# A prologue in pairs of token tiles, with attention units inside it, and a second norm in place on VectorE

## The chip, the cores and the metric

One core of a Trainium2 chip. The metric is the time on the device in microseconds, the median of several executions. The engines are named as in the profile: PE is TensorE's matmuls (PEld its weight loads), ACT is ScalarE, DVE is VectorE, POOL is GpSimd, SP is SyncE, which issues most of the DMAs.

## The reference

A block with S = 2048 tokens of D = 1024, 32 heads of 32, and an MLP of F = 3584 that gates the attention:

```python
xn = layernorm(x)                                     # first norm
q, k, v = split(xn @ wqkv)                            # 32 heads
s = softmax(q @ k.T * 32 ** -0.5) @ v @ wo            # "mha"
y = layernorm(xn)                                     # second norm
g = silu(gelu(y @ w1 + b1) @ w2 + b2)
out = x + s * g
```

Weights, inputs and the output are bfloat16.

## The kernel before

The kernel lists its operations in program order, and a small class finds for each the semaphores to wait on. What runs on one engine runs in the order of the list: the statistics of x stood on VectorE behind one small operation until 21.30 us.

The prologue works on four batches of four tiles of 128 tokens. All x tiles are loaded first, then the weights of K, Q and V for the first heads, and the halving of the bias `b2h` stands ahead of the statistics on VectorE:

```python
for tb in range(NT): ... dma_start(xst[tile tb], x2[tile tb])          # SyncE
load_wq(0)                                                             # three slices of 512 KB
...
op("gpsimd", dma_start(b2h, B_b2 ...), w=["b2"], dma="b2")
op("vector", tensor_scalar_mul(b2h, b2h, 0.5), r=["b2"], w=["b2"])
...
for tb in range(4): stat(tb)                     # two bn_stats and one bn_aggr, VectorE
for b in range(NT // 4):
    rstd(b); ...; nbias(b)                       # power of -1/2 on GpSimd
    for i in range(4): xnorm(4 * b + i) ...      # VectorE; between them stat of the next batch
    ycoef(b)                                     # small operations on GpSimd
    for i in range(4): ynorm(4 * b + i)          # GpSimd, then stored to DRAM
    for i in range(4): transp(4 * b + i)         # 8 transposes on TensorE, eviction to xnT on ScalarE
    run_now(qk_item(0, 1, 512 * b, 512)); ...    # K, four V, Q: 192 matmuls, evicted by ScalarE
load_piece(0); load_y(0)                         # first MLP weights; y, transposed by the DMA
```

(cut and shortened)

Then follow 512 attention units (8 groups of 4 heads, 8 query blocks, 8 key blocks). Each has 8 score matmuls, two exps of 128x1024 on ScalarE, and 16 matmuls for PV and the row sums. With each unit goes one *item* of other TensorE work, 28 to 32 matmuls: part of the MLP, a projection for the next heads, or, at the end, an output item (`wo_item`). The items share one PSUM bank, 7, so the next one starts only when the last one has been evicted by VectorE. Output items that are left after unit 511 run by themselves: the tail.

The softmax here doesn't subtract the row's maximum and nothing guards it: scores larger than these inputs give would overflow.

## Time and profile before

| | us |
|---|---|
| median of 4 runs (1173.06 to 1175.22) | 1173.76 |
| span of the profiled execution | 1170.1 |
| first exp / exp of unit 8 / exp of the last unit begin | 86.3 / 103.0 / 1131.0 |
| tail after the last exp begins | 39.1 |

The times of exps come from the trace's records of the 1024 exps in order; two make a unit, and the time given for a unit is the start of its first exp ("last" is unit 511). The page's row of 40 slices, each a fortieth of the span with its busy share in tenths, shows where there is slack:

```profile
PE   0789999999998999999999999999999999899998
ACT  0459999999999999999999999999999999999960
```

From the fourth slice on both engines are full, up to the tail. In the first slice TensorE does hardly anything, in the next two it is at 7 and 8 tenths, and ScalarE is not full before the fourth. The chain of waits, followed back from the last instruction to what each step waited for (start, duration, what; the kernel before), says why:

```profile
3.13 17.98 DMA b2h<-in_B_b_dram
21.13 0.17 DVE b2h L241
21.30 1.20 DVE stats L247 x2
...
38.34 9.40 PE ps L304 x145
48.37 3.72 ACT xnT L298 x4
52.13 8.83 PE ps L304 x192
...
90.25 1.94 ACT P L603 x2
...
1135.14 30.39 PE ps L304 x832
```

VectorE waits 18 us for the landing of a 4 KB bias, whose halving takes 0.17 us and whose result is needed only in the MLP; the statistics of x stand behind it. Projection begins at 38.34 us. Each batch then has matmuls, an eviction (left out), and 3.72 us in which ScalarE evicts the four transposed tiles; of these gaps of 4.4 us TensorE works for 1.9 (the transposes) and waits for 2.5. The last line is the tail: 26 output items of 32 matmuls, 1.17 us each.

The windows view gives the busy time of each engine in a stretch, with the count of instructions in brackets, then the granted clock, the DMA share and GB/s. Of the kernel before:

```profile
core 0: us, PE busy (x) PEld busy (x) DVE busy (x) ACT busy (x) POOL busy (x), PEclk, DMA share, GB/s
10.00:16.00 6.00, 0.00 (x0) 0.00 (x0) 0.00 (x0) 0.00 (x0) 0.00 (x0) 1.00 1.26 319
16.00:19.00 3.00, 0.00 (x0) 0.00 (x0) 0.00 (x0) 0.00 (x0) 0.00 (x0) 1.00 1.53 200
20.00:22.00 2.00, 0.00 (x0) 0.00 (x0) 0.87 (x3) 0.00 (x0) 0.00 (x0) 1.00 1.11 304
38.34:85.70 47.36, 39.79 (x868) 28.06 (x872) 19.36 (x36) 21.45 (x35) 22.22 (x29) 0.93 0.34 108
1131.45:1170.10 38.65, 34.78 (x960) 25.08 (x952) 31.13 (x63) 1.44 (x2) 0.73 (x1) 0.99 0.67 165
```

Three stretches of the front first: the DMAs move 319 GB/s while x (rows of 2 KB) loads, then 200 and 304 while the weights (rows of 512 bytes) do. In the projection TensorE is busy for 39.79 of 47.36 us at a clock of 0.93. One more reading is the group of the first normalizations on VectorE (line, operation, tile and shape, count; busy us, mean ns; idle before):

```profile
L279 DVE TENSOR_SCALAR hT<-OT,lnp 128x1024 bf16<-128x1024 bf16 x16 | 13.8, 880 | 6.2 <-PE ps L295 6.2
```

The mean of 880 ns mixes two kinds: some 500 ns, and 1170 ns (twice 1420) while GpSimd runs a `ynorm`.

### The profile page before, as it was taken

The numbers are of one execution on the slowest core, as the hardware profiler recorded it, in microseconds if no ns is written. First come the engines' busy times: TensorE is split into PE (matmuls) and PEld (weight loads), VectorE is DVE, ScalarE is ACT, GpSimd is POOL, SyncE is SP. The second block draws the span as 40 slices with busy tenths as digits, with TensorE's granted clock in tenths as the row PEclk, the third lists the DMA queues.
The fourth block names the chain that finished last, engine by engine and source line by source line (L and its number), as shares of the span: only waits on it lengthen the run. The fifth ranks groups of instructions, "written<-read, shape, count | busy, mean of one in ns | idle before, by whom it ended". The sixth has DMA issues, their size and how long they took to land.

```text
span 1170.1 us, 62673 instructions
## 1 busy us (share of the span) xinstructions
PE 1093.0 (93%) x29696; PEld 688.6 (59%) x29696; DVE 599.5 (51%) x1327; ACT 1054.9 (90%) x1281; POOL 88.2 (8%) x116
## 2 busy tenths in 40 slices
PE   0789999999998999999999999999999999899998
PEld 0555665566655666556666665566655566566666
DVE  2817665146682254764226675136673246742468
ACT  0459999999999999999999999999999999999960
POOL 1810000000000000000000000000000000000000
PEclk9999999999999999999999999999999999999999
DMA  9243226512245320433422225522145321752756
GB/s 198 110 122 105 62 80 170 161 60 75 75 125 159 113 80 4 146 102 103 133 64 77 76 87 144 174 87 76 51 127 155 115 72 50 227 150 78 134 139 173
DMA packets 198481, 129.87 MB, mean 111 GB/s; under 512 B 41552, under 2 KB 189008, under 8 KB 198224
## 3 DMA queue, kind: packets, MB, share of 16 engines
q1 hardware_dynamic: 193584, 125.85, 36.8%
q8 instruction: 232, 3.80, 1.3%
q0 software_dynamic: 4640, 0.02, 0.6%
q14 instruction: 25, 0.20, 0.1%
HBM read 104.87 MB, written 12.58 MB: 100 GB/s over the span
## 4 chain that ended last, share of the span: by engine, by line
PE 50%; ACT 42%; DVE 4%; DMA 3%; issue 2%; POOL 0%; SPq 0%; POOLq 0%
ACT P L603 37%; PE ps L304 30%; PE ps L591 8%; PE ps L620 7%; PE ps L623 5%; ACT th L404 3%; DMA b2h<-in_B_b_dram 2%; ACT xnT L298 1%; DMA war<-in_B_w_dram 1%; DVE stats L247 1%; DVE xb L396 1%; ACT thz L438 1%; DVE u L399 0%; DVE u L401 0%; DVE hT L279 0%
## 5 line engine op out<-in xcount | busy, mean ns | idle before, releaser
L603 ACT ACTIVATE P<-ps 128x1024 bf16<-128x1024 f32 x1024 | 984.6, 1103 | 18.7 <-PE ps L591 15.1
L620 PE MATMUL ps<-P,VP 128*32 128x256 bf16 x4096 | 262.9, 278 | 1.1 <-issue 1.0
L623 PE MATMUL ps<-P,ones 128*32 128x256 bf16 x4096 | 258.3, 273 | 1.6 <-issue 1.6
L304 PE MATMUL ps<-hT,war 128*32 128x352 bf16 (+1 forms) x5376 | 230.2, 308 | 8.6 <-issue 7.1
L304 PE MATMUL ps<-yTc,war 128*32 128x352 bf16 (+1 forms) x5376 | 225.9, 308 | 10.6 <-issue 5.0
L591 PE MATMUL ps<-QT,KT 32*128 32x256 bf16 x4096 | 204.2, 273 | 9.1 <-ACT P L603 5.1
L304 PEld LDWEIGHTS ps<-yTc,war 128*32 128x32 bf16 x5376 | 139.3, 97 | 57.8 <-issue 9.6
L620 PEld LDWEIGHTS ps<-P,VP 128*32 128x32 bf16 x4096 | 107.8, 95 | 111.0 <-issue 98.8
L304 PEld LDWEIGHTS ps<-hT,war 128*32 128x32 bf16 x5376 | 141.7, 97 | 50.7 <-issue 9.5
L396 DVE TENSOR_SCALAR xb<-ps,b1T 128x352 f32<-128x352 f32 (+1 forms) x168 | 96.1, 572 | 131.1 <-PE ps L304 130.1
L591 PEld LDWEIGHTS ps<-QT,KT 32*128 32x128 bf16 x4096 | 61.0, 92 | 155.6 <-ACT P L603 87.6
L304 PE MATMUL ps<-xnT,wq 128*32 128x352 bf16 (+2 forms) x2944 | 131.1, 321 | 9.2 <-ACT xnT L298 8.8
L643 POOL TENSOR_TENSOR OT<-accs,rcs 128x256 bf16<-128x256 f32 x64 | 53.0, 828 | 1022.5 <-DVE rcs L641 1022.5
L435 DVE TENSOR_SCALAR zh<-ps,b2h 128x352 f32<-128x352 f32 (+1 forms) x48 | 27.5, 573 | 180.2 <-PE ps L304 180.2
L623 PEld LDWEIGHTS ps<-P,ones 128*32 128x32 bf16 x4096 | 110.0, 96 | 3.7 <-issue 2.3
L408 DVE SCALAR_TENSOR_TENSOR hT<-th,xb 128x352 bf16<-128x352 f32 (+1 forms) x168 | 85.8, 511 | 37.7 <-ACT th L404 34.2
L304 PEld LDWEIGHTS ps<-xnT,wq 128*32 128x32 bf16 x2944 | 73.9, 98 | 42.0 <-ACT xnT L298 8.1
L404 ACT ACTIVATE th<-u 128x352 f32<-128x352 f32 (+1 forms) x168 | 97.4, 580 | 0.4
L399 DVE TENSOR_TENSOR u<-xb 128x352 f32<-128x352 f32 (+1 forms) x168 | 87.2, 519 | 0.2
L401 DVE SCALAR_TENSOR_TENSOR u<-u,xb 128x352 f32<-128x352 f32 (+1 forms) x168 | 82.9, 493 | 0.0
L304 PE MATMUL ps<-wq,xnT 128*32 128x256 bf16 x2048 | 66.7, 277 | 0.0
L634 DVE COPY accs<-ps 128x256 f32<-128x256 f32 x64 | 27.2, 424 | 67.9 <-PE ps L623 67.9
(44 smaller groups left out, 504.7 us busy)
## 6 DMA issues: line engine op xcount, KB each, us to landing
war<-in_B_w_dram SPq DMA_DIRECT2D x66, 1024.0 KB, 5.4
war<-in_B_w_dram SPq DMA_DIRECT2D x24, 768.0 KB, 5.4
wq<-in_A_wqkv_dram SPq DMA_DIRECT2D x12, 512.0 KB, 6.3
OT<-in_A_x_dram SPq DMA_DIRECT2D x16, 256.0 KB, 6.2
y_scratch<-hT SPq DMA_DIRECT2D x16, 256.0 KB, 2.0
xnT<-in_A_x_dram SPq DMA_DIRECT2D x16, 256.0 KB, 3.9
out_dram<-wq SPq DMA_DIRECT2D x16, 256.0 KB, 2.5
gT_scratch<-gst SPq DMA_DIRECT2D x40, 88.0 KB, 1.7
```

The costliest lines, as they stand in the source:

```text
L304: ins = e.matmul(outs(j), lhsT=lhs(j), rhs=rhs, start=start, stop=stop, tile_position=(0, 32 * j), skip_group_check=True)
L396: op("vector", lambda e: e.tensor_scalar(xb[:, 0:n], bank(bk, 0, n), b1T[:, f:f + 1], None, op0=ALU.add), r=[("b", bk), "b1"], w=[kx])
L399: "vector", lambda e: e.tensor_tensor(ub[:, 0:n], xb[:, 0:n], xb[:, 0:n], op=ALU.mult), r=[kx], w=[ku]))
L401: "vector", lambda e: e.scalar_tensor_tensor(ub[:, 0:n], ub[:, 0:n], 1.0 / 0.044715, xb[:, 0:n], op0=ALU.add, op1=ALU.mult),
L404: "scalar", lambda e: e.activation(th[:, 0:n], ub[:, 0:n], ACT.Tanh, scale=0.7978845608028654 * 0.044715),
L408: "vector", lambda e: e.scalar_tensor_tensor(hT[:, f, 0:n], th[:, 0:n], 1.0, xb[:, 0:n], op0=ALU.add, op1=ALU.mult),
L435: op("vector", lambda e: e.tensor_scalar(zh[:, 0:n], bank(bk, 0, n), 0.25, b2h[:, nb:nb + 1], op0=ALU.mult, op1=ALU.add), r=[("b", bk), "b ...
L591: ins = e.matmul(bank(bks[j], kh * 256, (kh + 1) * 256), lhsT=KT[i2][32 * j:32 * j + 32, k0:k0 + 128], rhs=QT[i2][32 * j:32 * j + 32, qb * ...
L603: op("scalar", lambda e, p=p, sl=sl: e.activation(pb[:, 2 * p:2 * p + 2, :, :].rearrange("p a b q -> p (a b q)"), ps[:, sl * 1024:(sl + 1) ...
L620: e.matmul(bankq(ACC, j, 0, QW), lhsT=VP[vp][:, kb, vo + 32 * j:vo + 32 * j + 32], rhs=pb[:, j, kh, :], start=first, stop=False, tile_posi ...
L623: ins = e.matmul(bankq(ACC, j, QW, 2 * QW), lhsT=ones[:, 0:32], rhs=pb[:, j, kh, :], start=False, stop=last, tile_position=(0, 32 * j), sk ...
L643: op("gpsimd", lambda e: e.tensor_tensor(OT[:, hg, qb * QW:(qb + 1) * QW], a[:], rc[:], op=ALU.mult), r=[ka, kr], w=[("OT", hg, qb), ("xst ...
```

## The change

Three intentions: take the bias out of VectorE's way; work in pairs of tiles, so that the transposes of the next pair run between the matmuls of this one; and begin the attention within the prologue, pair p being followed by unit p. The second norm moves from GpSimd to VectorE, in place in the x tile, and most of it to units 8 to 20. The core of the diff:

```diff
-        load_wq(0)                                    # behind all 16 x tiles
+        load_x(0); load_x(1)
+        load_wq(0, (1,))                              # K
+        load_x(2); load_x(3)
+        load_wq(0, (0, 2))                            # Q, V
+        for tb in range(4, NT): load_x(tb)
-        op("vector", lambda e: e.tensor_scalar_mul(b2h[:], b2h[:], 0.5), r=["b2"], w=["b2"])
         ...
         def ynorm(tb):
-            op("gpsimd", lambda e: e.tensor_scalar(ybb[i], xst[...], ...))
+            op("vector", lambda e: e.tensor_scalar(xt, xt, ...))              # in place
         ...
+        def pre_pair(p):                              # statistics run one pair ahead
+            stat(2 * p + 2); nbias(p); xnorm(2 * p); xnorm(2 * p + 1)
+            stat(2 * p + 3); rstd(p + 1); ycoef(p)
+            transp(2 * p); transp(2 * p + 1)
+        def pro_unit(p):
+            pre_pair(p + 1)
+            if p < 3: ynorm(p)
+            pair_kq(p); pair_v(p)                     # 64 + 64 matmuls, evicted by ScalarE
         ...
         while u < NU + 2 ...:
+            if u < NP: pro_unit(u)                    # NP = 8 pairs
+            elif u == NP: ...tensor_scalar_mul(b2h, b2h, 0.5)
+            if u == 4: load_piece(0); load_y(0)
             s_unit(u) ... exp_unit(u) ... pv_unit(u - 2)
-            if state["qi"] < total:                   # one item with each unit
+            if u >= NP and state["qi"] < total:       # none with units 0 to 7
                 ...
+                if NP <= u < NP + NT - 3: ynorm(u - NP + 3)
                 it.finish(...)                        # eviction of the item bank
```

(cut; in units 0 to 7 the scores use the same four banks each time, instead of a rotation over six)

More of the change, by code (lines that the diff above doesn't have):

```diff
@@ L204, in bass_recurrent_scan__mha_block__mixer_channel_mlp__prompt_kernel @@
         xnb = [hflat[:, i * D:(i + 1) * D] for i in range(4)]
-        ybb = [hflat[:, (4 + i) * D:(5 + i) * D] for i in range(4)]
         xst = OT[:].rearrange("p g s -> p (g s)")
@@ L222, in bankb, with load_x @@
             return ps[:, i * 512:(i + 1) * 512].bitcast(BF16)
-        for tb in range(NT):
-            op("sync", lambda e, tb=tb: e.dma_start(xst[:, tb * D:(tb + 1) * D], x2[tb * 128:(tb + 1) * 128, :]),
+        def load_x(tb):
+            op("sync", lambda e: e.dma_start(xst[:, tb * D:(tb + 1) * D], x2[tb * 128:(tb + 1) * 128, :]),
                w=[("xst", tb)], dma=f"x{tb % 8}")
@@ L232, in load_wq @@
                 op("sync", lambda e, src=src, t3=t3: e.dma_start(wq[:, t3, :, :], src), w=[("wq", t3)], dma=f"wq{t3}")
-        load_wq(0)
+        load_x(0)
+        load_x(1)
+        load_wq(0, (1,))
+        load_x(2)
+        load_x(3)
+        load_wq(0, (0, 2))
+        for tb in range(4, NT):
+            load_x(tb)
         op("gpsimd", lambda e: e.iota(iota_i[:], pattern=[[1, 128]], base=0, channel_multiplier=-1), w=["iota"])
@@ L252, in rstd @@
         def rstd(b):
-            lo, hi = 4 * b, 4 * b + 4
+            lo, hi = 2 * b, 2 * b + 2
             L = lambda k: lnp[:, k, lo:hi]
@@ L256, in rstd @@
             op("vector", lambda e: e.tensor_scalar_add(L(0), mv[:, lo:hi, 1], EPS), r=mvk, w=[("l0", b)])
-            op("gpsimd", lambda e: e.tensor_tensor(L(2), L(0), mhalf[:], op=ALU.pow), r=[("l0", b), "mhalf"], w=[("l2", b)])
+            op("gpsimd", lambda e: e.tensor_tensor(L(2), L(0), mhalf[:, 0:2], op=ALU.pow), r=[("l0", b), "mhalf"], w=[("l2", b)])
         def nbias(b):
-            lo, hi = 4 * b, 4 * b + 4
+            lo, hi = 2 * b, 2 * b + 2
             L = lambda k: lnp[:, k, lo:hi]
@@ L266, in ycoef @@
         def ycoef(b):
-            lo, hi = 4 * b, 4 * b + 4
+            lo, hi = 2 * b, 2 * b + 2
             L = lambda k: lnp[:, k, lo:hi]
@@ L272, in ycoef @@
             op("gpsimd", lambda e: e.tensor_scalar(L(4), L(4), 1.0, EPS, op0=ALU.mult, op1=ALU.add), r=[("l4", b)], w=[("l4", b)])
-            op("gpsimd", lambda e: e.tensor_tensor(L(5), L(4), mhalf[:], op=ALU.pow), r=[("l4", b), "mhalf"], w=[("l5", b)])
+            op("gpsimd", lambda e: e.tensor_tensor(L(5), L(4), mhalf[:, 0:2], op=ALU.pow), r=[("l4", b), "mhalf"], w=[("l5", b)])
             op("gpsimd", lambda e: e.tensor_tensor(L(6), L(2), L(5), op=ALU.mult), r=[("l5", b), ("l2", b)], w=[("l6", b)])
@@ L280, in xnorm, with pro_bank @@
                                                    op0=ALU.mult, op1=ALU.add),
-               r=[("xst", tb), ("l2", tb // 4), ("l3", tb // 4)], w=[("xnb", i)])
+               r=[("xst", tb), ("l2", tb // 2), ("l3", tb // 2)], w=[("xnb", i)])
         def ynorm(tb):
-            i = tb % 4
-            op("gpsimd", lambda e: e.tensor_scalar(ybb[i], xst[:, tb * D:(tb + 1) * D], lnp[:, 6, tb:tb + 1], lnp[:, 7, tb:tb + 1],
-                                                   op0=ALU.mult, op1=ALU.add),
-               r=[("xst", tb), ("l6", tb // 4), ("l7", tb // 4)], w=[("ybb", i)])
-            op("sync", lambda e: e.dma_start(y_d[tb * 128:(tb + 1) * 128, :], ybb[i]), r=[("ybb", i)], w=[("y", tb)], dma=f"yst{i}")
+            xt = xst[:, tb * D:(tb + 1) * D]
+            op("vector", lambda e: e.tensor_scalar(xt, xt, lnp[:, 6, tb:tb + 1], lnp[:, 7, tb:tb + 1], op0=ALU.mult, op1=ALU.add),
+               r=[("xst", tb), ("l6", tb // 2), ("l7", tb // 2)], w=[("xst", tb)])
+            op("sync", lambda e: e.dma_start(y_d[tb * 128:(tb + 1) * 128, :], xt), r=[("xst", tb)], w=[("y", tb)], dma=f"yst{tb % 4}")
+        pro_banks = [4, 5, 7]
+        pbk = {"n": 0}
+        def pro_bank():
+            pbk["n"] += 1
+            return pro_banks[(pbk["n"] - 1) % 3]
         def transp(tb):
-            i, bk = tb % 4, tb % 4
+            i, bk = tb % 4, pro_bank()
             def f(e):
@@ L313, in __init__, with qk_item @@
                 self.steps, self.finish, self.parts, self.pre = steps, finish, parts, pre
-        def qk_item(hg, which, t0, n, ev="vector"):
+        def qk_item(hg, which, t0, n):
             i2, co = hg % 2, (hg % 2) * 128
@@ L325, in fin, with v_item @@
             def fin(bk):
-                keys = [(nm, i2, t) for t in toks(t0, n)]
-                if ev == "vector":
-                    op("vector", lambda e: e.tensor_copy(dst[:, t0:t0 + n], bank(bk, 0, n)), r=[("b", bk)], w=keys)
-                else:
-                    op("scalar", lambda e: e.activation(dst[:, t0:t0 + n], bank(bk, 0, n), ACT.Copy), r=[("b", bk)], w=keys)
+                op("vector", lambda e: e.tensor_copy(dst[:, t0:t0 + n], bank(bk, 0, n)), r=[("b", bk)],
+                   w=[(nm, i2, t) for t in toks(t0, n)])
             return Item([lambda bk, dc=dc: step(dc, bk) for dc in range(DC)], fin)
-        def v_item(hp, tb, ev="vector"):
+        def v_item(hp, tb):
             i2 = hp % 2
@@ L342, in fin @@
             def fin(bk):
-                if ev == "vector":
-                    op("vector", lambda e: e.tensor_copy(VP[i2][:, tb, :], bank(bk, 0, 256)), r=[("b", bk)], w=[("VP", i2, tb)])
-                else:
-                    op("scalar", lambda e: e.activation(VP[i2][:, tb, :], bank(bk, 0, 256), ACT.Copy), r=[("b", bk)], w=[("VP", i2, tb)])
+                op("vector", lambda e: e.tensor_copy(VP[i2][:, tb, :], bank(bk, 0, 256)), r=[("b", bk)], w=[("VP", i2, tb)])
             return Item([lambda bk, dc=dc: step(dc, bk) for dc in range(DC)], fin)
@@ L405, in fin @@
                     r=[ku], w=[kt]))
-                extra = [("xnb", i) for i in range(4)] + [("ybb", i) for i in range(4)] if c == 0 else []
+                extra = [("xnb", i) for i in range(4)] if c == 0 else []
                 dve_tasks[u + 3].append(lambda: op(
@@ L488, in wo_item @@
             return Item([lambda bk, hc=hc: step(hc, bk) for hc in range(HG)], fin, pre=pre)
-        pbk = {"n": 0}
-        def run_now(it):
-            bk = 4 + pbk["n"] % 4
-            pbk["n"] += 1
-            if it.pre:
-                it.pre()
-            for s in it.steps:
-                s(bk)
-            it.finish(bk)
-        for tb in range(4):
-            stat(tb)
-        for b in range(NT // 4):
-            rstd(b)
-            if b + 1 < NT // 4:
-                stat(4 * b + 4)
-            nbias(b)
-            for i in range(4):
-                xnorm(4 * b + i)
-                if i < 3 and b + 1 < NT // 4:
-                    stat(4 * b + 5 + i)
-            ycoef(b)
-            for i in range(4):
-                ynorm(4 * b + i)
-            for i in range(4):
-                transp(4 * b + i)
-            run_now(qk_item(0, 1, 512 * b, 512, ev="scalar"))
-            for i in range(4):
-                run_now(v_item(0, 4 * b + i, ev="scalar"))
-            run_now(qk_item(0, 0, 512 * b, 512, ev="scalar"))
@@ L522, in bass_recurrent_scan__mha_block__mixer_channel_mlp__prompt_kernel, with pair_kq, f @@
-        load_piece(0)
-        load_y(0)
+        NP = NT // 2
+        def pair_kq(p):
+            t0, bk = 256 * p, pro_bank()
+            def f(e):
+                for which, off in ((1, 0), (0, 256)):
+                    for dc in range(DC):
+                        ins = mm4(e, lambda j: bankq(bk, j, off, off + 256), lambda j: wq[:, which, dc, 32 * j:32 * j + 32],
+                                  xnT[:, dc, t0:t0 + 256], dc == 0, dc == DC - 1)
+                return ins
+            op("tensor", f, r=[("wq", 0), ("wq", 1), ("xnT", 2 * p), ("xnT", 2 * p + 1)], w=[("b", bk)])
+            for nm, dst, off in (("KT", KT, 0), ("QT", QT, 256)):
+                op("scalar", lambda e, dst=dst, off=off: e.activation(dst[0][:, t0:t0 + 256], bank(bk, off, off + 256), ACT.Copy),
+                   r=[("b", bk)], w=[(nm, 0, 2 * p), (nm, 0, 2 * p + 1)])
@@ new lines, in pair_v, with f @@
+        def pair_v(p):
+            bk = pro_bank()
+            def f(e):
+                for i in range(2):
+                    t0 = (2 * p + i) * 128
+                    for dc in range(DC):
+                        ins = mm4(e, lambda j: bankq(bk, j, 256 * i, 256 * i + 256), lambda j: xnT[:, dc, t0 + 32 * j:t0 + 32 * j + 32],
+                                  wq[:, 2, dc, :], dc == 0, dc == DC - 1)
+                return ins
+            op("tensor", f, r=[("wq", 2), ("xnT", 2 * p), ("xnT", 2 * p + 1)], w=[("b", bk)])
+            op("scalar", lambda e: e.activation(VP[0][:, 2 * p:2 * p + 2, :].rearrange("p a n -> p (a n)"), bank(bk), ACT.Copy),
+               r=[("b", bk)], w=[("VP", 0, 2 * p), ("VP", 0, 2 * p + 1)])
@@ new lines, in pre_pair @@
+        def pre_pair(p):
+            more = p + 1 < NP
+            if more:
+                stat(2 * p + 2)
+            nbias(p)
+            xnorm(2 * p)
+            xnorm(2 * p + 1)
+            if more:
+                stat(2 * p + 3)
+                rstd(p + 1)
+            ycoef(p)
+            transp(2 * p)
+            transp(2 * p + 1)
+        stat(0)
+        stat(1)
+        rstd(0)
+        pre_pair(0)
+        def pro_unit(p):
+            if p + 1 < NP:
+                pre_pair(p + 1)
+            if p < 3:
+                ynorm(p)
+            pair_kq(p)
+            pair_v(p)
@@ L552, in bass_recurrent_scan__mha_block__mixer_channel_mlp__prompt_kernel @@
                     proj.append([(v_item(hv, vts[i]), 0, DC)])
-            end = len(flat) + UPH
+            end = (hg + 1) * UPH - NP
             lead = 4
@@ L576, in bass_recurrent_scan__mha_block__mixer_channel_mlp__prompt_kernel, with slot @@
                 flat.append((wo_item(tb, k), 0, HG))
+        def slot(u, p):
+            return p if u < NP else (2 * u + p) % 3
         def s_unit(u):
@@ L584, in s_unit @@
             for j in range(4):
-                bks.append(2 * ((2 * u + j // 2) % 3) + j % 2)
+                bks.append(2 * slot(u, j // 2) + j % 2)
             def f(e):
@@ L601, in exp_unit @@
             for p in range(2):
-                sl = (2 * u + p) % 3
+                sl = slot(u, p)
                 op("scalar", lambda e, p=p, sl=sl: e.activation(
@@ L653, in bass_recurrent_scan__mha_block__mixer_channel_mlp__prompt_kernel @@
             cur["u"] = u
+            if u < NP:
+                pro_unit(u)
+            elif u == NP:
+                op("vector", lambda e: e.tensor_scalar_mul(b2h[:], b2h[:], 0.5), r=["b2"], w=["b2"])
+            if u == 4:
+                load_piece(0)
+                load_y(0)
             if u < NU:
@@ L678, in bass_recurrent_scan__mha_block__mixer_channel_mlp__prompt_kernel @@
                     t()
+                if NP <= u < NP + NT - 3:
+                    ynorm(u - NP + 3)
                 if hi == len(it.steps):
```

## The prediction

> **What bounds it now.** From 100 to 200 us the windows view shows ScalarE busy 100.0 and TensorE 99.0 of 100 us: an attention unit is two exps (1.83 us) and a share of tanh on ScalarE; scores, PV and one item (about 2.05) on TensorE. Little is to be had there. The slack is in the first 86 us. In the chain of waits VectorE waits from 3.1 to 21.1 us for the bias b2h, whose multiply stands ahead of all statistics. Projection runs on TensorE from 38.3 to 85.7 us, busy 39.8 of 47.4, granted clock 0.93, with waits for evictions of xnT. No exp runs before 86.3 us. After the last unit (1131 us), 26 output items drain on TensorE alone, 30.39 us, 1.17 each.
>
> **What the change does.**
> 1. The b2h wait leaves the front. x and wq still take until about 20 us (some 325 GB/s while x streams, 200 while wq does, by the windows). With x0, x1, K weights, x2, x3, Q and V weights ahead of x4, I estimate x4 at 14 to 15 us; VectorE needs it before it normalizes tile 2. First projection: about 17.7 us instead of 38.3.
> 2. Pairs. Estimate per pair on TensorE: K and Q 1.74, V 1.74 (V evictions come 0.87 us apart), 16 transposes 0.98, scores 0.4, PV 0.55: 5.4 us. ScalarE: xnT 1.86, K and Q 0.7, V 0.6, exps 1.84: about 5. VectorE: statistics 2.8, normalizations 0.9, ynorm 0.45: about 4. So TensorE-bound, 5.5 to 6 us per pair, ScalarE close behind.
> 3. The exps of units 0 to 7 run inside the projection. The exp of unit 8, at 103.2 us now, should start at about 66: 37 us earlier.
> 4. Given back: units 0 to 7 carry no item, so 8 output items move from attention to the tail: 8 x 1.17 = 9.4 us. Units 8 to 20 carry a ynorm of 0.45 us on VectorE ahead of the eviction of the single item bank: a loss of 2 us. Another 0.5 for tanh.
> 5. The 16 ynorms of 1.22 us leave GpSimd. While they run, normalizations on VectorE take 1.17 us instead of 0.50.[...] In a TensorE-bound prologue this only keeps VectorE ahead.
>
> Net: 37 - 9.4 - 2.5 = 25, on the critical path.
>
> **Prediction.** 1149 us; 8 in 10 between 1141 and 1158. Faster by over 2% 0.57, within 2% 0.42, slower 0.01. The 2% line, 1150.3, is almost at my centre.
>
> **What will show it.** Chain of waits: no b2h; start limited by x and wq to some 15-17 us. First projection matmul at 16 to 20 us, eighth scores at 60 to 66, exp of unit 8 at 65 to 71. Normalizations near 0.5 us. Then 2.0 to 2.1 us per unit, as before; last exp about 35 us earlier; tail about 9 us longer, with 34 output items.
>
> **What would make it wrong.** (a) Pairs at 7 us, because scores wait for exps in the same banks (no rotation there), or TensorE pauses and its clock drops[...]; the K projection at 38.3 took 3.6 us, warm 1.9[...]. That costs 8 to 10 us: about 1158. (b) wq in 512-byte rows delays x2 to x5 more than I think, 3 us. (c) ynorm delays evictions more, up to 5 us. (d) Pairs at 5.3 us: about 1147.

The sum: 37 - 9.4 - 2.5 = 25 us, from 1173.76 to 1149. What the trace of the kernel before does show is a granted clock of 0.50 for 3.41 us, twice in the projection, within 1.1 us after a wait of TensorE of 2.5 us (experiment 11). The times per pair in step 2 are estimates from durations in that trace: on TensorE 1.91 us for the 32 K or Q matmuls of four tiles, 1.96 for 32 transposes, 0.40 for the scores, 0.61 for PV and sums; on ScalarE 0.93 for an eviction to xnT, 0.60 for K or Q of four tiles, 0.38 for V of one, 0.92 for an exp; on VectorE 1.20 and 0.21 for the statistics of a tile, 0.42 to 0.55 for a normalization, the figure also taken for a ynorm there. The 2 and 0.5 us in step 4 are estimates.

## The result, and the profile after

| | before | after |
|---|---|---|
| median (lowest to highest), us | 1173.76 (1173.06 to 1175.22) | 1142.92 (1142.65 to 1149.03) |
| span of the profiled execution | 1170.1 | 1140.6 |
| first projection matmul | 38.3 | 18.9 |
| first exp / exp of unit 8 / of unit 20 / last | 86.3 / 103.0 / 127.1 / 1131.0 | 23.7 / 65.2 / 91.4 / 1092.2 |
| last exp to the end | 39.1 | 48.4 |

The ratio is 0.9748, with a 95% interval of 0.9714 to 0.9782. Ratios here are the mean time of one kernel's fast runs over that of the other's of the same rounds, so not quite the ratio of the medians. The difference of the medians is 30.8 us, that of the spans 29.5 us; the profiled execution of the kernel before was itself 1.9 us under its median. The slices of the kernel after:

```profile
PE   4999999999999999999999999999999999899998
ACT  3889999999999999999999999999999999899930
```

TensorE is full from the second slice on; ScalarE is at 8 tenths there and full from the fourth, as before. The chain of waits of the kernel after:

```profile
5.60 9.23 DMA OT<-in_A_x_dram
...
17.05 1.89 PE ps L306 x16
18.93 4.24 PE ps L315 x124
...
48.73 3.61 PE ps L315 x128
52.34 0.33 PE ps L623 x8
...
53.22 1.00 PE ps L306 x16
54.22 3.61 PE ps L315 x128
...
62.85 1.84 ACT P L635 x2
...
1096.41 39.61 PE ps L315 x1086
```

The bias is gone. The front now waits for x tile 4 (9.23 us), and projection starts at 18.93 us. The lines from 48.73 to 54.22 show one pair in the steady state: 128 projection matmuls 3.61 us, scores 0.33, PV and sums (left out), transposes 1.00, the next 128 matmuls. Pair follows pair at 5.49 us with nothing but TensorE in the chain. At the end of the prologue it goes through ScalarE once: the scores of unit 8 wait for the exps of unit 7. The last line is the tail, 34 items. Windows of the kernel after:

```profile
core 0: us, PE busy (x) PEld busy (x) DVE busy (x) ACT busy (x) POOL busy (x), PEclk, DMA share, GB/s
18.87:62.13 43.26, 41.37 (x1257) 34.79 (x1256) 23.22 (x60) 34.03 (x51) 17.81 (x48) 1.00 0.36 93
1092.70:1140.60 47.90, 44.02 (x1220) 32.41 (x1208) 39.25 (x79) 1.46 (x2) 0.74 (x1) 0.99 0.74 173
```

From the first projection to the scores of unit 7 TensorE is busy for 41.37 of 43.26 us, attention units included, at full clock from 20.2 us on, where the clock's records begin (the first 128 matmuls took 4.24 us, later ones 3.61). The normalizations, now without ynorms on GpSimd beside them:

```profile
L284 DVE TENSOR_SCALAR hT<-OT,lnp 128x1024 bf16<-128x1024 bf16 x12 | 6.0, 544 | 1.0 <-PE ps L306 0.8
```

544 ns, two in a row, instead of a mean of 880.

The ledger of the spans, each from the two rows of exp times above:

| stretch | before | after | difference | predicted |
|---|---|---|---|---|
| start to exp of unit 8 | 103.03 | 65.19 | -37.8 | -37 |
| exp of unit 8 to unit 20 | 24.10 | 26.25 | +2.2 | +2.5 |
| exp of unit 20 to the last | 1003.82 | 1000.78 | -3.0 | 0 |
| last exp to the end | 39.15 | 48.38 | +9.2 | +9.4 |
| sum | 1170.1 | 1140.6 | -29.5 | -25 |

Three of the four terms are within a microsecond. The experiments ask what the first term is made of, whether the overlap in it is worth anything, and what the third term is. The third, of the long stretch from the exp of unit 20 to the last, varies from kernel to kernel (experiment 9), so it helps to look at the other three terms together, that is at the span without the long stretch: 166.3 us before and 139.8 after.

### The profile page after: what moved, and what is told of

It is laid out like the page before. It is cut to its first block, busy times and chain, and to the rows that moved or that the text cites. A ratio compares the mean times of both kernels' runs of the same rounds, so it can differ in the third digit from the quotient of the medians.

```text
span 1140.6 us, 63237 instructions
## 1 busy us (share of the span) xinstructions
PE 1091.3 (96%) x29952; PEld 695.6 (61%) x29952; DVE 603.6 (53%) x1351; ACT 1053.7 (92%) x1281; POOL 77.0 (7%) x128
## 4 chain that ended last, share of the span: by engine, by line
PE 65%; ACT 27%; DVE 4%; DMA 2%; issue 1%; SPq 0%
PE ps L315 38%; ACT P L635 25%; PE ps L623 10%; PE ps L652 10%; PE ps L655 6%; ACT th L409 2%; DMA war<-in_B_w_dram 1%; DVE xb L401 1%; DMA OT<-in_A_x_dram 1%; DVE u L404 1%; PE ps L306 1%; DVE u L406 0%; DVE hT L413 0%; ACT thz L443 0%; DVE accs L666 0%
## 5 line engine op out<-in xcount | busy, mean ns | idle before, releaser
L315 PEld LDWEIGHTS ps<-yTc,war 128*32 128x32 bf16 x5376 | 139.9, 97 | 58.4 <-issue 7.1
L315 PE MATMUL ps<-xnT,wq 128*32 128x352 bf16 (+2 forms) x3200 | 128.3, 304 | 2.3 <-DVE xb L401 2.1
L675 POOL TENSOR_TENSOR OT<-accs,rcs 128x256 bf16<-128x256 f32 x64 | 53.1, 830 | 1001.7 <-DVE rcs L673 1001.7
L315 PEld LDWEIGHTS ps<-xnT,wq 128*32 128x32 bf16 x3200 | 79.9, 97 | 29.5 <-DVE xb L401 3.2
L666 DVE COPY accs<-ps 128x256 f32<-128x256 f32 x64 | 27.2, 424 | 67.7 <-PE ps L655 67.7
```

Source lines behind the costliest of these rows:

```text
L315: ins = e.matmul(outs(j), lhsT=lhs(j), rhs=rhs, start=start, stop=stop, tile_position=(0, 32 * j), skip_group_check=True)
L675: op("gpsimd", lambda e: e.tensor_tensor(OT[:, hg, qb * QW:(qb + 1) * QW], a[:], rc[:], op=ALU.mult), r=[ka, kr], w=[("OT", hg, qb), ("xst ...
```

## The experiments

Eleven kernels ran; all gave the reference's result. "Exp 8" is the start of the exp of unit 8 in the profiled execution. Ratios are against the kernel before of the same rounds.

| | kernel | median (range), us | ratio (95%) | exp 8 |
|---|---|---|---|---|
| 1 | before, bias halved later | 1156.22 (1154.76 to 1158.90) | 0.9848 (0.9826 to 0.9869) | 86.3 |
| 2 | after, bias halved early | 1160.94 (1160.03 to 1163.52) | 0.9889 (0.9870 to 0.9908) | 80.2 |
| 3 | after, pairs first, no overlap | 1142.93 (1141.74 to 1144.83) | 0.9734 (0.9716 to 0.9751) | 75.0 |
| 4 | after, x0 to x5 ahead of weights | 1140.44 (1133.70 to 1143.70) | 0.9705 (0.9661 to 0.9749) | 59.5 |
| 5 | 1 with the new order of loads | 1161.09 (1159.17 to 1161.93) | 0.9889 (0.9870 to 0.9908) | 92.7 |
| 6 | after, all ynorms in the pairs | 1148.55 (1147.75 to 1149.92) | 0.9781 (0.9764 to 0.9798) | 66.3 |
| 7 | after, ynorm on GpSimd | 1145.81 (1144.37 to 1149.42) | 0.9761 (0.9738 to 0.9784) | 64.8 |
| 8 | after, new front and 6 | 1140.71 (1138.97 to 1142.45) | 0.9713 (0.9692 to 0.9733) | 61.4 |
| 9 | after, 64 TensorE instructions more | 1144.71 (1143.84 to 1146.55) | 0.9743 (0.9721 to 0.9765) | 66.1 |
| 10 | after, first MLP loads later | 1147.00 (1146.23 to 1149.51) | 0.9763 (0.9743 to 0.9783) | 64.4 |
| 11 | 4 and output weights later | 1137.32 (1133.41 to 1141.88) | 0.9673 (0.9647 to 0.9699) | 59.8 |

### 1. The bias alone, in the kernel before

```diff
-        op("vector", ...tensor_scalar_mul(b2h[:], b2h[:], 0.5)...)      # ahead of the statistics
         ... (the whole prologue)
+        op("vector", ...tensor_scalar_mul(b2h[:], b2h[:], 0.5)...)
         load_piece(0)
```

> The kernel before, with one line moved: the halving of b2h stands after the prologue instead of ahead of the statistics. Theory A (the wait for b2h is on the critical path of the front): statistics start at about 4 us, the first projection matmul at about 21 us (when the K weights have landed behind x) instead of 38.3, and the time falls by 15 to 18 us, to about 1157. Theory B (x and wq take until 20 us anyhow, and the gain of the change comes from running attention units inside the projection): the first projection moves by 5 us at most and the time stays above 1168.

Measured: first projection at 21.63 us, 1156.22 us. Its chain of waits:

```profile
10.90 10.69 DMA wq<-in_A_wqkv_dram
21.63 9.40 PE ps L303 x183
```

The K weights, at the end of the queue of loads, now hold the front. From there the kernel runs just as before, 16.7 us earlier at the exp of unit 8 and 17.0 us earlier at the last. So one moved line is worth 17 of the 30 us, and theory B is refuted: the loads take until about 22 us either way, but the statistics, normalizations and transposes of the first batch (transposes from 11.3 to 19.3 us here) run while they come in.

### 2. The bias put back, in the changed kernel

```diff
+        op("vector", ...tensor_scalar_mul(b2h[:], b2h[:], 0.5)...)      # behind the load of b2h
         ...
-            elif u == NP: ...tensor_scalar_mul(...)
```

> The changed kernel, with the halving of b2h put back ahead of the statistics. Theory A: statistics start at 21 us, the first projection at about 32 instead of 18.9, the time rises by 12 to 14 us, to about 1156. Theory B: it rises by 3 us at most.

Measured: 1160.94 us, 18 us more, so theory A again, but the size was missed. The bias landed at 22.7 us, the first projection came at 34.0 us and exp 8 15.0 us later than in the changed kernel; the other 3.6 us were lost later, by unit 511. The first part missed by a little, as the bias landed 1.6 us later than in the kernel before. Of the second part 1.6 us lie between the exps of units 8 and 20, where one of TensorE's half-clock stretches falls (granted clock 0.50 for 3.4 us, at 80.5 us). After that a second one, at 206.8 us, explains nothing, since the changed kernel has one too (972.5 us); but TensorE's pauses without a releaser (nothing that the profile shows ended them; see experiment 9) are 2.1 us longer in sum.

### 3. Pairs without overlap

```diff
+        for p in range(NP):
+            pro_unit(p)
+            if p == 4: load_piece(0); load_y(0)
         ...
-            if u < NP: pro_unit(u)
-            if u >= NP and state["qi"] < total:
+            if state["qi"] < total:
```

(and the score banks and the list of items as in the kernel before)

> The changed kernel with all eight pairs first and unit 0 of the attention after them, its items given to units 0 to 511 as before. Theory A (TensorE time counts: units 0 to 7 inside the projection save their 2.05 us each, but cost 0.9 us of TensorE each there, and 1.17 us for each of the 8 items that go to the tail, which is nothing on balance): pairs at about 4.6 us, first exp at 56 to 58 us instead of 86.3, tail of 26 output items again, and the time is 1143 to 1148, within 5 us of the changed kernel. Theory B (the overlap of exps with projection is what pays): 1157 or more, that is 14 us or more of the gain lost.

Measured: 1142.93 us against 1142.92 for the changed kernel. The chain of waits of this kernel at the end of its prologue:

```profile
44.89 1.00 PE ps L306 x16
45.89 3.61 PE ps L315 x128
49.50 1.00 PE ps L306 x16
...
57.60 0.33 PE ps L630 x8
```

Pairs take 4.60 us here (44.89 to 49.50), 0.89 us less than with an attention unit inside. First exp at 58.15 us, and the tail has 26 items again: 39.1 us from the last exp instead of 48.4. The span without the long stretch is 139.8 us in both kernels. So the overlap, which looks like the heart of the change, brings nothing. TensorE's account says why: in the changed kernel units 0 to 7 cost 8 x 0.89 = 7.1 us inside the pairs, and their items 9.2 us in the tail, 16.3 together; here the eight units with their items take 16.9 us (exps from 58.15 to 75.03). Work was moved from one full stretch of TensorE to another. ScalarE's exps did move to where ScalarE was idle, but beyond the prologue it was no scarcer than TensorE.

What pays beside the bias is thus the pipeline: from experiment 1 to this one projection starts 2.6 us earlier (21.6 to 19.1) and lasts 38.5 instead of 47.4 us, since the normalizations and evictions of the next pair run beneath the matmuls of this one. The three changes of batch took 13.2 us, and six transposes of pairs take 6.0 in their place; two half-clock stretches of 3.4 us (granted clock 0.50) at such changes went as well, an estimated 1.7 us each, half their length (they remain in the trace of experiment 1). The new loads and the ynorm on VectorE came with the pairs; of these only the loads were tried alone (experiment 5).

### 4. More x tiles ahead of the weights

```diff
-        load_x(0); load_x(1); load_wq(0, (1,)); load_x(2); load_x(3); load_wq(0, (0, 2))
-        for tb in range(4, NT): load_x(tb)
+        for tb in range(6): load_x(tb)
+        load_wq(0, (1, 0, 2))
+        for tb in range(6, NT): load_x(tb)
```

> The changed kernel with x tiles 0 to 5 loaded ahead of all three weight slices. If the 9.2 us wait for x tile 4 in the chain of waits is what holds the first projection: VectorE is no longer held, the first projection matmul comes at 15 to 16 us instead of 18.9, and the time falls by 3 to 4 us, to about 1139.5. If the K weights then hold it as long, no change (within 1 us).

Measured: first projection at 14.6 us, exp 8 5.7 us earlier, the last exp 3.8 us earlier; the median falls by 2.5 us, with runs from 1133.7 to 1143.7. The wait for x tile 4 did hold the front. How much of the 5.7 us arrives at the end varies from run to run more than the effect is large, so the size is seen in the trace only: the span without the long stretch falls by 5.7 us, to 134.1, and in the long stretch, with two half-clock stretches instead of one, 1.9 us are lost again.

### 5. The new order of loads in the old batches

```diff
 (experiment 1, and)
-        for tb in range(NT): load_x(tb)
-        load_wq(0)
+        load_x(0); load_x(1); load_wq(0, (1,)); load_x(2); load_x(3); load_wq(0, (0, 2)); ...
```

> The kernel before with the halving of b2h moved and, beside it, the new order of loads (x0, x1, K weights, x2, x3, Q and V weights, then the other x), but still batches of four tiles and no overlap. With b2h moved alone the first projection waited for the K weights until 21.6 us. Theory A: now it comes at 19 us, held by the normalizations on VectorE, and the time falls by about 2.5 us against that kernel, to 1153 to 1154; what then separates it from all pairs first (1143) is the finer pipeline. If the order of loads matters more than that, x4 late (14 us) delays the statistics of the second batch: then no gain, about 1156.

Measured: the second outcome, and worse: 1161.09 us, 4.9 us over experiment 1. The timeline of VectorE in this kernel (start, duration, operation; in brackets the idle time before it and what ended it):

```profile
15.99 1.29 DVE L253 BATCH_NORM_STATS2 stats<-OT 128x6 f32<-128x512 bf16 x2 [3.80 <-DMA OT<-in_A_x_dram]
```

These are the statistics of x tile 4. In the old order of operations they stand ahead of all normalizations of the first batch, so a late x4 delays everything: first projection at 27.2 us instead of 21.6. So the new order of loads is no gain of its own; the changed kernel pays for it too (experiment 4), and gains in spite of it.

### 6. All second norms in the pairs

```diff
-            if p < 3: ynorm(p)
+            ynorm(2 * p); ynorm(2 * p + 1)
         ...
-                if NP <= u < NP + NT - 3: ynorm(u - NP + 3)
```

> The changed kernel with two ynorms in each pair of the prologue and none in the attention. If the ynorms in units 8 to 20 delay the evictions of the item bank: the stretch from the exp of unit 8 to that of unit 20 takes 24.1 us as in the kernel before, instead of 26.25, pairs stay at 5.5 us (VectorE has about 5.1 us of work per pair), and the time falls by about 2 us. If VectorE becomes the limit of the pairs, these take longer than 5.5 us, and the gain is lost.

Measured: from exp 8 to exp 20 25.29 us, against 26.25 in the changed kernel and 24.10 before. So the ynorms explain 1.0 us of the 2.2 us lost there; the rest fits the first items themselves, MLP items in a row, each with a tanh on ScalarE (in the kernel before such units come 2.21 us apart from 90.25 us on, later ones 2.02), but no run separates it. The pairs stayed at 5.49 us, but two pauses of TensorE of 1.5 and 0.9 us came in (at 47.7 and 53.1 us), and the time rose by 5.6 us where I expected 2 less. Of that, 1.1 us stand at exp 8 and 5.0 us come after unit 20, where the account of experiment 9 finds 5.1 us more of pauses and half clock. The span without the long stretch is 139.9 us, against 139.8, so the edit itself cost nothing and brought nothing. The expectation failed; the ynorms in units 8 to 20 are a small cost.

### 7. The second norm on GpSimd

```diff
-            op("vector", lambda e: e.tensor_scalar(xt, xt, ...))
+            op("gpsimd", lambda e: e.tensor_scalar(xt, xt, ...))
```

> The changed kernel with the in-place ynorm on GpSimd instead of VectorE, in the same places. If VectorE's work is what delays units 8 to 20: from the exp of unit 8 to that of unit 20 24.1 to 25 us instead of 26.25. [...]some VectorE operations with SBUF operands (squares, products) stretch by up to 1 us while a ynorm of 1.2 us runs, and the stretch takes as long as now or longer. Time within 2 us of the changed kernel either way.

Measured: 28.93 us from exp 8 to exp 20, 2.7 us more than in the changed kernel: as long as in the second outcome, but not by its cause, as it turns out. The timeline of VectorE in this kernel, and its GpSimd, which runs eight ynorms back to back:

```profile
75.14 1.44 DVE L406 SCALAR_TENSOR_TENSOR u<-u,xb 128x352 f32<-128x352 f32 x1
76.50 0.52 DVE L404 TENSOR_TENSOR u<-xb 128x352 f32<-128x352 f32 x1
76.94 0.51 DVE L337 CAST KT<-ps 128x352 bf16<-128x352 f32 x1
...
73.18 12.22 POOL L290 TENSOR_SCALAR OT<-OT,lnp 128x1024 bf16<-128x1024 bf16 x8
```

The cube of the MLP (a product of two SBUF tiles) takes 1.44 us here (694 ns in the mean from exp 8 to exp 20, against 500 in the changed kernel); the eviction of K from PSUM, which also ran beside a ynorm, takes 0.51 as ever. Not every operation with SBUF inputs is held (the square between them took 0.52, one at 72.5 us 1.06), and what decides it is not shown. But the 2.7 us lost are not these longer operations. From exp 8 to exp 20 TensorE waited only 0.4 us for VectorE here, against 1.2 in the changed kernel, and had two pauses without a releaser, 1.2 and 2.0 us (at 71.4 and 82.6 us), where the changed kernel had none. So which engine is the better place for the second norm is not shown; the medians' intervals overlap too.

### 8. A combination

```diff
-        (loads as in the change)
+        x0 to x3, K weights, x4, Q weights, x5, x6, V weights, x7 to x15
         def pro_unit(p):
+            if p == 0: pair_kq(p)                # ahead of the transposes of pair 1
             ...
 (and experiment 6)
```

> The changed kernel with three things: x tiles 0 to 4 ahead of the Q weights and 5 and 6 ahead of the V weights; the K and Q projection of the first pair before the transposes of the second; all ynorms in the pairs. First projection at 11.5 to 12.5 us instead of 18.9; exp of unit 8 at 57 to 58 us instead of 65.2; from there to unit 20 24.1 us instead of 26.25. In all 8 to 10 us less than the changed kernel: 1133 to 1136. If VectorE cannot keep up with two ynorms per pair, 1137 to 1140.

Measured: 1140.71 us, no better than experiment 4. The first projection did come at 12.9 us, held by the Q weights, but its 64 matmuls took 3.56 us, where the same group takes 1.93 later, and the scores of unit 0 came at 19.2 us, against 18.9 in experiment 4: beginning sooner gained nothing. The ynorms in the pairs brought as little as in experiment 6.

### 9. The same work with 64 more TensorE instructions

```diff
-                for dc in range(DC):
+                for dc in list(range(DC)) * (5 if tb == 1 else 1):       # same transposes, repeated
                     ins = e.transpose(...)
```

> The changed kernel with the eight transposes of x tile 1 made five times over (64 more TensorE instructions, weight loads counted, in the 5 us in which TensorE idles before 17 us; same result, nothing else moves). Open is why the stretch from the exp of unit 20 to the last took 3.0 us less after the change (1000.8 against 1003.8 us). Theory C: TensorE sometimes runs out of instructions, because a 16 KB packet of its instruction queue comes late behind bulk loads; where such packets fall depends on the count of instructions before. Then the waits put down to no releaser in the long stretch move to other places and their sum changes, and the stretch changes by 1 us or more. Theory D: the stretch is set by which item meets which unit: then waits and stretch stay as in the changed kernel, within 0.5 us.

TensorE's waits from the exp of unit 20 to the last (total us, times, longest). Before, then after, then this kernel:

```profile
PE ps L304 <- issue: 12.2, 12, 1.8
PE ps L304 <- DVE xb L396: 4.5, 11, 0.7
```

```profile
PE ps L315 <- issue: 8.2, 11, 1.3
PE ps L315 <- DVE xb L401: 5.3, 12, 0.7
```

```profile
PE ps L315 <- issue: 8.3, 15, 1.1
PE ps L315 <- DVE xb L401: 4.9, 11, 0.7
```

"issue" is time in which the engine waited for nothing that the profile shows. In items it is 4 us less after the change than before; the waits for the eviction of the item bank are about equal. In this kernel the long stretch takes 1001.4 us against 1000.8, and the sum for "issue" in items is again 8.3 us, but in 15 pauses instead of 11, and the pauses of 0.4 us and more lie in part elsewhere: up to 400 us they are at 147, 177, 187, 310 and 316 us in the changed kernel, and at 101, 206, 315 and 347 here. With the lines of scores and PV the sums for "issue" are 16.3, 11.4 and 13.2 us. So both theories fail in part: places and the whole sum moved, as C says, while the length stayed within 0.6 us, nearly as D says.

The traces settle more than this run does. Count TensorE's recorded instructions (matmuls, weight loads and its sequencer's waits) from the start: all 184 pauses of at least 0.4 us without a releaser, in the thirteen kernels, stand at a count that leaves 192 or 193 when divided by 256 (below: at an edge; 15 of them in the kernel before, 14 in the changed one), and each ends 2.2 to 2.9 us after the start of a 16 KB packet of TensorE's instruction queue, one of which comes for every 256 instructions (232 for 59392 before, 234 for 59904 after); in the median such a packet starts some 3.7 us before TensorE reaches the edge. In the 3 us before those packets the other DMAs moved 347 GB/s in the median, and over 200 before 183 of them; before the other packets 30 in the median, and over 200 before a third. In the traces of the kernels before and after, the packets of the 29 pauses started 0.45 to 1.93 us before TensorE stopped at the edge; of the 436 others 404 started 2 us or more before it was reached. So the records fit theory C, that TensorE stands still there for its next instructions, whose packet comes late behind bulk loads; that it waits for the packet is read from these times, and no record shows the wait itself. Why not every packet behind bulk loads is late stays open.

The same account gives the length of the stretch. Pauses without a releaser, waits for MLP weights and half of the half-clock time (an estimate of what is lost there, from the granted clock of 0.50; in the kernel before 32 matmuls of K took 3.47 us at 76.9 us, nearly all at that clock, and 1.91 at full clock) are 18.4 us before and 14.9 after, and 13.7 to 20.0 in the thirteen kernels; what is left of the stretch is 984.3 to 986.5 us in all of them.

The inserted transposes also cost 1 us at the front: the clock fell to half from 16.8 to 23.6 us.

### 10. The first MLP loads later

```diff
-            if u == 4: load_piece(0); load_y(0)
+            if u == 6: load_piece(0, after=<TensorE's last operation>); load_y(0)
```

> The changed kernel with the first load of MLP weights (1 MB) and the transposed load of y issued in unit 6 of the prologue, not as soon as y is stored (29 us). Theory C: the 1.4 us pause of TensorE inside a group at 34.7 us, which has no releaser, goes away or moves to 53 to 60 us, with the loads. If the pause has nothing to do with the loads it stays at 34 to 36 us. Time within 2 us of the changed kernel.

In the changed kernel TensorE stands still in the middle of a group of matmuls, without a releaser. Windows view, the changed kernel:

```profile
core 0: us, PE busy (x) PEld busy (x) DVE busy (x) ACT busy (x) POOL busy (x), PEclk, DMA share, GB/s
34.70:36.00 1.30, 0.00 (x0) 0.00 (x0) 1.30 (x4) 1.30 (x2) 1.08 (x3) 1.00 0.25 32
```

and this kernel:

```profile
core 0: us, PE busy (x) PEld busy (x) DVE busy (x) ACT busy (x) POOL busy (x), PEclk, DMA share, GB/s
34.70:36.00 1.30, 1.30 (x42) 0.66 (x31) 1.25 (x5) 0.87 (x2) 1.14 (x2) 1.00 0.05 13
```

The pause is gone here. TensorE stands still for 1.4 us at 64.9 us instead, followed by a half-clock stretch (0.51 from 66.2 to 69.7 us), but that wait has a releaser, the moved load of y (chain of waits of this kernel):

```profile
57.59 8.64 DMA yTc<-y_scratch
```

So the pause went away with the loads, as theory C expected, and did not move with them. The trace's packet records fit theory C: TensorE's instruction queue moves 16 KB packets, 234 of them for 59904 TensorE instructions, one per 256; in the changed kernel one came at 27.1 us and the next only at 33.6, in this one at 26.6, 31.4 and 35.4. So this pause goes with the bulk loads, and it is one of the 184 of experiment 9, at an edge. The time did not gain: y landed at 66.2 us, too late for the first item, and it took 1147.00 us.

### 11. A version that beats both

```diff
 (experiment 4, and)
-                if state["qi"] == q_end: ...; load of wo (2 MB)
+                if state["qi"] == q_end: ...
+                if state["qi"] == q_end + 24: load of wo
```

> The changed kernel with x tiles 0 to 5 ahead of the weights (as in the fourth experiment) and the 2 MB load of the output weights 24 items later. In the changed kernel that load stands in front of an MLP weight piece at 960 us: TensorE pauses for 1.3 and 1.8 us and then runs 3.4 us at half clock. Expected: both pauses and the half clock go, 4 to 5 us beside the 2.5 us of the loads: 1134 to 1137. If the MLP pieces are late by themselves (1 MB per 8 us), only 1 us beside the loads: 1139.

The changed kernel at the time when the output weights load (windows view):

```profile
core 0: us, PE busy (x) PEld busy (x) DVE busy (x) ACT busy (x) POOL busy (x), PEclk, DMA share, GB/s
967.00:972.50 5.50, 2.37 (x68) 1.29 (x60) 3.67 (x8) 4.48 (x7) 0.85 (x1) 1.00 0.88 293
972.50:975.90 3.40, 3.40 (x68) 2.01 (x60) 1.62 (x4) 1.22 (x2) 0.00 (x0) 0.50 0.53 188
```

TensorE works for 2.37 of 5.5 us there (a pause of 1.3 us without a releaser, and a wait of 1.8 us for an MLP weight piece that stands behind the 2 MB), and then has half its clock, 0.50, for 3.40 us. In the kernel before, three waits of 2.5 us (at 49.6, 62.8 and 74.4 us) were followed by a clock of 0.50 for 3.41 us after the first and the third (from 53.2 and 77.1 us), not after the second. So which pauses bring the half clock is not shown. This kernel at the same work:

```profile
core 0: us, PE busy (x) PEld busy (x) DVE busy (x) ACT busy (x) POOL busy (x), PEclk, DMA share, GB/s
962.00:967.00 5.00, 4.23 (x132) 2.72 (x124) 4.37 (x10) 5.00 (x9) 0.85 (x1) 1.00 0.53 161
967.00:972.00 5.00, 4.77 (x148) 3.15 (x138) 4.02 (x11) 5.00 (x8) 0.00 (x0) 1.00 0.16 56
```

The two long pauses and the half clock are gone there. The median is 1137.32 us, and the interval of its ratio (0.9647 to 0.9699) lies wholly below that of the changed kernel (0.8% less time); it overlaps that of experiment 4, so what the later load adds is seen in the trace only. In the profiled execution the last exp begins 1.5 us earlier than in experiment 4: part of the gain was lost again in three pauses of 1.4 to 1.8 us without a releaser, between 988 and 1012 us, of which only the last falls into the moved load. The expected 1134 to 1137 was just missed.

## Why the prediction was right, and where its sum was off

The predicted 1149 us and the measured 1142.92 us differ by 6 us; the range held it, and "faster" was the likelier class.

1. *The bias leaves the front; first projection at about 17.7 us, held by x4 at 14 to 15.* Right: x4 at 14.9, first projection at 18.9. (The 200 GB/s "while wq does" I had put down to the rows of wq; they come from those rows and the 4-byte packets of the biases beside them, together.) Experiment 1 shows its worth, 17 us, and experiment 4 that x4 held it.
2. *Pairs bound by TensorE at 5.5 to 6 us.* Right: 5.49 us, with only TensorE in the chain. The feared drop of the clock (granted 1.00) and the wait for score banks did not come, apart from the 1.65 us ahead of unit 8.
3. *Exp of unit 8 at 66 us.* Right: 65.2.
4. *Given back: 9.4 us in the tail, 2.5 us in units 8 to 20.* Right in size, 9.2 and 2.2 us. The split was off: I gave ynorm 2 us and the items 0.5; experiment 6 shows 1.0 for ynorm, so 1.2 for the rest.
5. *ynorm leaves GpSimd, normalizations at 0.5 us.* 0.54 us. That it only keeps VectorE ahead is consistent with pairs bound by TensorE; that it would cost more on GpSimd is not shown (experiment 7).

The term that was mis-sized is one that I had set to zero, "then 2.0 to 2.1 us per unit, as before": from unit 20 on the stretch took 3.0 us less, with 4 us less of TensorE's pauses without a releaser. By the account of experiment 9 the pauses, waits for weights and half clock in it fell by 3.5 us, from 18.4 to 14.9, and that is the whole of it. In twelve kernels with nearly the same work there (before, after, and experiments 1 to 10) this stretch takes 1000.8 to 1005.7 us, and the changed kernel has the lowest figure; experiment 9 shows that 64 instructions at the front are enough to move its pauses. So I count it as scatter that a change of the instruction stream brings; by theory C, which the records fit, it decides which packets of instructions meet bulk loads. The prediction did not aim at this gain, and that it came out as a gain is luck. Another 1.3 us are the difference between medians and profiled spans.

The net was right while one thing was not said: the 37 and the 9.4 us contain the same work twice. The prediction put the gain of the overlap into the first and its cost into the fourth step, and did not see that they cancel (experiment 3).

## What to carry to other kernels

When two engines are both full, draw up the account of the busier one before overlapping anything: moving its work from one full stretch to another brought nothing here (1142.93 against 1142.92 us, experiment 3), however idle the second engine was. Look first at what stands at the head of an engine's list; one moved line, an operation of 0.17 us that waited 18 us for a DMA, gave more than half of this gain. And a change in the order of loads has to be judged with the order of operations that wait for them: the same order cost 4.9 us in batches.
